# The second row of q is added by the DMA that loads it, in a pooled attention and gated FFN kernel

## Chip, cores and metric

The kernel runs on one core of one Trainium2 chip. The metric is the device time of one execution in microseconds. The engines are named as the profile names them: PE (TensorE, matmuls), DVE (VectorE), ACT (ScalarE), POOL (GpSimd) and SP (SyncE, which here issues DMAs and computes nothing). Each engine works through its own list of instructions in order; between engines there are only semaphores.

## What is computed

Attention over 4 batches of 8 heads, 1152 keys, head width 64. Two neighbouring queries are averaged first, so 576 pooled queries are left. Its output goes through a small network with a convolution of three taps as a gate. Cut to what matters:

```python
q_pool = q.reshape(B, H, S // 2, 2, D).mean(axis=3)
scores = q_pool @ k.T / sqrt(D)
attn = softmax(scores)            # with 1e-9 added to the sum
x = (attn @ v) -> (B, 576, 512)
h = relu(x @ w_in)                # 512 -> 1024
conv = w0 * h[t-1] + w1 * h[t] + w2 * h[t+1]
out = (h * sigmoid(conv)) @ w_out # 1024 -> 512
```

The change touches the first of these lines: the mean of two neighbouring rows of q, which the kernel makes as a sum (the factor is folded into a later scale).

## The kernel before

The 32 heads are worked on as 16 pairs (`Pair`, two heads share the 128 partitions). For each pair, `loads` brings in k, q and v from DRAM with DMAs that SP issues. q lies in DRAM in a layout in which the two queries of a mean stand as two rows of 640 columns beside each other, so one load fills the tile `qin` of 128 x 2 x 640 floats. There is one copy of `qin` in on-chip memory (`r_qin` has one slot), so a pair's load can start only when the pair before has been read.

`sum_q` (L299) adds row 1 of `qin` into row 0; it is a task of POOL, or of DVE where the table `SWAPPED` names it. Then ACT reads row 0 three times: `keep_q` (L302) makes `qt`, and two `turn_q` (L306) make `qd`, the copy with the two halves of the partitions exchanged. The score matmuls (L455) read `qt`, `qd` and `kt`.

`softmax` handles five blocks of 128 queries for each pair, with two score tiles for each of the first four and one for the last: 144 tiles in all, two of which fit in PSUM. For each tile: PE makes the scores (L455), DVE the row maximum (L467), ACT the exponential with its sum (L472), ACT or DVE the denominators (L485, L489), DVE the reciprocal (L495). Then the probabilities are scaled and split into two f16 halves: the high half on ACT (L519) or POOL (L514), the low half on DVE (L522), and a DMA transposes them (L535). For a few heads the scaling keeps f32 (L553 on ACT, L557 on POOL or DVE) and PE transposes (L571), ACT copies (L576). `values` multiplies with v (L601, L607), and v itself is split beforehand (L387 on POOL, L392 on ACT, L395 on DVE). `feed` is the first layer with relu, taps and gate (L691 to L725), `second` the second layer (L899 to L911) and its store. The weights come as 64-bit words and are decoded at the start and along the way by `weights` (L988 to L1044).

The order of all this is not made by dependences but by hand-carried tables: every step is a `Task`, `ORDER` lists the numbers of all 2484 tasks in the order in which they are emitted (so every engine's own order follows from it), `SLOTS` says which copy of a buffer each taker uses, and `SWAPPED` which tasks go to their second engine.

Of the kernel before, what the change touches and what calls it, by code (L numbers as in the profile page):

```python
# [94 lines left out]
cYaacXcZc2c4bNauc3c5c0abacadaehTafagc6ahc7c8hWhUc9bOdnc1aihVhXavibajawbPhYaEaxdmayiehZh0azh8ich1aAh9dbh2idaBia  # L95
h6ifh3aCitaFigaGdadqdJaHihiwdsiiaIaDiuiqh4dtakdrdOaJixijh5dHaKd0h7aLiyikirimdciLaMalivamanddaoaNiOapaOdKaqdGiz
ardLiAiMilasdMioiniBatdfiPiIipaYiNiEiJaPi3dNaQiFd1dgaRiQiKdhaSiGdiaTiRaZiSi4iCi0aUjrisdja0dka1i1iDi5a2i6joiTi7
dla3iHjba4iWjpi2d4iUiXjsjeiVdejqiYa5aVjtjGaWiZjJjui8jva6jHjDjcbijfd6jgaXi9a7jKjIjajEd5a8dobjjYdpjwjLjFbkbljdj1
bmjMjhd7bnjNjzjZbojVeneGjBjAjCjxj2jOjkjya9jWduj0bpj3babbdvj4j5bckdbqjTbdkgbrkedwbEjXkjjUkhj6bejPjldxeqjRkkjQki
dzdAbfj7klkybgdBj8dCdDjSj9kzdEkberkTkmdFkAkndIkvkUkfbFkWkBkakokwkLkceskCbGkXkDetbheHbHd8kGdykVbskEkHkMkIkJbtkY  # L100
kxlbbubIbvkZbJbyk0lek1lck8krkKdPkFkpksbwlfkqktd3k6kufAldk9k2bKltbxlglabQk3lwdQbRlhbSk7k4lilubTljkPbAbUlqlxbVk5
lvdRlrdSb5bCbzlolylslLbDlplzlOkQlAbLlMlIlBdTlmb6dUeKlPlElnlFlClkdVlDb7lNlJlGlQl3b8lKdWb9lHlRmolScalldXlTl0l4ep
# [1113 lines left out]
```

## Time and profile before

| | us |
|---|---|
| runs of the kernel before | 639.64, 641.41, 645.65 (median 641.41) |
| the execution that was profiled | 639.12 |
| its span, from first to last instruction | 637.3 |
| PE busy in it | 579.9 |
| DVE busy | 578.0 |
| ACT busy | 522.2 |
| POOL busy | 170.9 |

The span is the time between the first and the last instruction of the profiled execution; 1.8 us of its time lie around the span. "Busy" is the time in which an engine executes something other than register, semaphore and DMA-issuing instructions. An engine that waits is not busy, but an engine that is not the bottleneck may wait at no cost, so the shares are read stretch by stretch.

### The profile page before, as it was taken

The page shows a single profiled execution, that of the slowest core. Times are in us where ns is not written, and L with a number is a line of the kernel's source. Part 1 is how long each engine was busy: PE and PEld are TensorE (multiplying, and loading weights), DVE is VectorE, ACT ScalarE, POOL GpSimd, SP SyncE. Part 2 cuts the span into 40 slices and gives each one's busy share as a digit, 9 for nine tenths or more (in the row PEclk, how much of TensorE's full clock was granted, in tenths as well). Part 3 has the DMA queues.
Part 4 walks back from the last instruction along what each step waited for, and adds up shares of the span by engine and source line. Part 5 has one row for each costly group of instructions (what it writes and reads, how often), then busy time and mean ns, then how long its engine had stood idle before and what let it go on. Part 6 is the DMA issues. An engine that isn't in the chain of part 4 may idle for free. (4 is left out here: it accounts for less than half of the span.)

```text
span 637.3 us, 11886 instructions
## 1 busy us (share of the span) xinstructions
PE 579.9 (91%) x4411; PEld 361.6 (57%) x4411; DVE 578.0 (91%) x934; ACT 522.2 (82%) x982; POOL 170.9 (27%) x170
## 2 busy tenths in 40 slices
PE   3768888889999899999999899999999889999897
PEld 1435554556666565546666566475566536667753
DVE  5999999999999999989998999999999999987871
ACT  6999999969998888877888898678878788966761
POOL 0342434441313321033221211423121311231110
PEclk9779999889999999999999999999999999999999
DMA  7899696956386698999997999999999988988601
GB/s 271 257 185 197 163 213 144 209 119 140 84 191 163 159 185 166 189 186 188 221 199 170 225 191 178 176 209 189 191 166 239 180 144 159 197 135 133 90 34 42
DMA packets 276970, 109.63 MB, mean 172 GB/s; under 512 B 264880, under 2 KB 265904, under 8 KB 276912
## 3 DMA queue, kind: packets, MB, share of 16 engines
q1 hardware_dynamic: 276912, 108.87, 83.4%
q8 instruction: 35, 0.57, 0.4%
q14 instruction: 23, 0.19, 0.1%
HBM read 37.77 MB, written 4.72 MB: 67 GB/s over the span
## 5 line engine op out<-in xcount | busy, mean ns | idle before, releaser
L455 PE MATMUL s<-kt,qt 64*128 64x512 f32 (+3 forms) x704 | 190.5, 488 | 29.1 <-ACT p L472 20.2
L472 ACT ACTIVATE p<-s,sm 128x1152 f32<-128x1152 f32 x144 | 175.3, 1218 | 33.4 <-DVE sm L467 17.5
L467 DVE TENSOR_REDUCE sm<-s 128x1 f32<-128x1152 f32 x144 | 192.7, 1347 | 6.6 <-PE s L455 6.4
L522 DVE SCALAR_TENSOR_TENSOR hl<-p,sm,hl 128x1152 f16<-128x1152 f32 (+1 forms) x116 | 165.6, 1435 | 7.5 <-ACT hl L519 4.7
L455 PEld LDWEIGHTS s<-kt,qt 64*128 64x128 f32 (+1 forms) x704 | 91.9, 178 | 133.0 <-issue 80.2
L455 PE MATMUL s<-kt,qd 64*128 64x512 f32 x256 | 147.4, 657 | 0.0
L514 POOL TENSOR_SCALAR hl<-p,sm 128x1152 f16<-128x1152 f32 (+1 forms) x50 | 72.5, 1450 | 185.0 <-DVE sm L495 132.1
L601 PE MATMUL a<-pt,v 128*64 128x256 f16 (+2 forms) x1566 | 119.7, 272 | 1.9 <-DMA pt<-hl 1.2
L691 PE MATMUL a<-x,wi 128*128 128x257 f16 (+3 forms) x864 | 105.3, 274 | 4.6 <-ACT pt L576 1.5
L519 ACT ACTIVATE hl<-p,sm 128x1152 f16<-128x1152 f32 (+1 forms) x66 | 82.2, 1251 | 21.1 <-DVE sm L495 13.5
L601 PEld LDWEIGHTS <-v 128*64 128x64 f16 x1566 | 91.2, 110 | 11.3 <-issue 4.8
L691 PEld LDWEIGHTS <-wi 128*128 128x128 f16 x864 | 76.9, 98 | 30.6 <-issue 10.3
L905 PE MATMUL a<-wo,g 128*128 128x512 f32 x160 | 74.0, 602 | 0.4 <-DVE vs L353 0.4
L715 DVE SCALAR_TENSOR_TENSOR g<-h,cw,g 128x255 f32<-128x255 f32 (+3 forms) x144 | 68.8, 497 | 4.4 <-ACT g L704 3.9
L607 PE MATMUL a<-pt,v 128*64 128x256 f32 (+1 forms) x252 | 64.1, 409 | 0.7 <-ACT pt L576 0.7
L571 PE MATMUL a<-ident,p 128*128 128x128 f32 (+1 forms) x315 | 48.7, 281 | 15.2 <-POOL p L557 4.8
L576 ACT ACTIVATE pt<-a 128x384 f32<-128x384 f32 (+2 forms) x98 | 44.6, 475 | 7.3 <-PE a L571 7.3
L571 PEld LDWEIGHTS a<-ident,p 128*128 128x128 f32 (+1 forms) x315 | 32.8, 144 | 29.3 <-ACT pt L576 9.3
L905 PEld LDWEIGHTS a<-wo,g 128*128 128x128 f32 x160 | 28.7, 190 | 30.4 <-issue 28.4
L708 POOL TENSOR_SCALAR g<-h,cw 128x255 f32<-128x255 f32 (+3 forms) x26 | 22.5, 868 | 74.9 <-ACT h L697 53.3
L697 ACT ACTIVATE h<-a,bs 128x257 f32<-128x257 f32 (+3 forms) x72 | 33.6, 470 | 9.5 <-PE a L691 6.3
L557 POOL TENSOR_SCALAR p<-p,sm 128x1152 f32<-128x1152 f32 (+1 forms) x17 | 24.5, 1444 | 58.9 <-DVE sm L495 42.8
(134 smaller groups left out, 668.1 us busy)
## 6 DMA issues: line engine op xcount, KB each, us to landing
qin<-in_q_dram SPq DMA_DIRECT2D x15, 640.0 KB, 4.9
kt<-in_k_dram SPq DMA_DIRECT2D x16, 576.0 KB, 5.5
vin<-in_v_dram SPq DMA_DIRECT2D x9, 576.0 KB, 4.1
g<-in_moe_w_in_dram SPq DMA_DIRECT2D x8, 512.0 KB, 5.1
w<-in_moe_w_out_dram SPq DMA_DIRECT2D x8, 512.0 KB, 4.1
out_dram<-o SPq DMA_DIRECT2D x16, 256.0 KB, 2.7
vin<-in_v_dram SPq DMA_DIRECT2D x7, 288.0 KB, 3.2
v<-in_v_dram SPq DMA_DIRECT2D x7, 288.0 KB, 3.5
```

Of the source, the lines that this page charges most:

```text
L455: nc.tensor.matmul(out=w, lhsT=f, rhs=kk, start=True, stop=True)
L467: nc.vector.tensor_reduce(out=sm[:, e:e + 1], in_=runs(st[e]), axis=AX.XY, op=ALU.max, negate=True)
L472: nc.scalar.activation(out=p.tile().rearrange("p (a n) -> p a n", a=2), in_=runs(st[e]), func=AF.Exp, bias=sm[:, e:e + 1], scale=1.0, accu ...
L514: eng.tensor_scalar(out=hl[rows, 0], in0=ps_[e][rows], scalar1=sm[rows, 6 + e:7 + e], scalar2=1.0, op0=ALU.mult, op1=ALU.mult,)
L519: nc.scalar.activation(out=hl[rows, 0], in_=ps_[e][rows], func=AF.Copy, scale=sm[rows, 6 + e:7 + e])
L522: nc.vector.scalar_tensor_tensor(out=hl[rows, 1], in0=ps_[e][rows], scalar=sm[rows, 6 + e:7 + e], in1=hl[rows, 0], op0=ALU.mult, op1=ALU.s ...
L571: nc.tensor.transpose(w[:, (i - a1) * nq:(i - a1 + 1) * nq], ps_[e][rows, i * P:(i + 1) * P], ident[rows, rows])
L601: nc.tensor.matmul(out=to, lhsT=o.v[:, e, c, vc:vc + D], rhs=o.pt[y, e][:, hl * NC + c, 0:n], start=(c == 0 and j == 0), stop=(c == NC - 1 ...
L607: nc.tensor.matmul(out=to, lhsT=o.v[:, e, c].bitcast(F32), rhs=p32.rearrange("p (a n) -> p a n", a=NC)[:, c, 0:n], start=(c == 0), stop=(c ...
L691: nc.tensor.matmul(out=w[:, 0:n], lhsT=wi[:, a, j, f * P:(f + 1) * P], rhs=x.x[:, c, s0:s0 + n], start=(i == 0 and j == 0), stop=(i == 2 a ...
L715: nc.vector.scalar_tensor_tensor(out=c, in0=h[:, t:t + tok], scalar=cw[:, f, t:t + 1], in1=c, op0=ALU.mult, op1=ALU.add)
L905: nc.tensor.matmul(out=w.tile(), lhsT=g[f // 4][:, f % 4, c:c + P], rhs=wo[:, f, :], start=(f == 0), stop=(f == FC - 1),)
```

## The change

For pairs 1 to 15 SP now loads only row 0 of q (320 KB instead of 640 KB). The sum is no instruction of DVE or POOL any more: POOL issues a DMA that loads row 1 and adds it to row 0 in on-chip memory. Pair 0, whose q comes in two parts at the very start, keeps its two loads and sums. The tables `ORDER`, `SLOTS` and `SWAPPED` are new throughout, since the order was searched again. In `split_out`, which borrows `qin` late in the program, the shape of the borrowed tile is written in another way; its instructions are the same.

```diff
         def load_q(cols):
-            nc.sync.dma_start(
-                out=o.qin.tile()[:, :, cols], in_=q[o.pr].rearrange("p (r n) -> p r n", r=2)[:, :, cols]
-            )
+            rows = q[o.pr].rearrange("p (r n) -> p r n", r=2)
+            if o is pairs[0]:
+                nc.sync.dma_start(out=o.qin.tile()[:, :, cols], in_=rows[:, :, cols])
+            else:
+                nc.sync.dma_start(out=o.qin.tile()[:, 0, cols], in_=rows[:, 0, cols])
...
+        def add_q(cols):
+            nc.gpsimd.dma_start(
+                out=o.qin[:, 0, cols], in_=q[o.pr].rearrange("p (r n) -> p r n", r=2)[:, 1, cols], accum_op=ALU.add
+            )
...
-            t = add("POOL", 0.2 + 1.32 * n / K0, lambda eng, cols=cols: sum_q(eng, cols), after=[lq[i]], uses=[o.qin],
-                    port=True, alt=("DVE", dve(n), True))
+            if o is pairs[0]:
+                t = add("POOL", 0.2 + 1.32 * n / K0, lambda eng, cols=cols: sum_q(eng, cols), after=[lq[i]], uses=[o.qin],
+                        port=True, alt=("DVE", dve(n), True))
+            else:
+                t = add("POOL", 1.1, lambda sum_q=add_q, cols=cols: sum_q(cols), after=[lq[i]], uses=[o.qin], dma=1.5)
...
-cYaacXcZc2c4bNauc3c5c0abacadaehTafagc6ahc7c8hWhUc9bOdnc1aihVhXavibajawbPhYaEaxdmayiehZh0azh8ich1aAh9dbh2idaBia
+cYaacXc2cZc4auc0dmbNabc1c3acc5adaehTafagc6ahc7c8hWaihUc9avdnajhXhVaEawhYibaxayhZh0h8h1ieicbOdbh9idh2dqazh6iaif
```

How many instructions of each kind stand on an engine before and after, counted in the two built programs (kinds that are not listed are equal; lines are those of the kernel before):

| engine | kind | before | after |
|---|---|---|---|
| POOL | sum of q L299 | 9 | 0 |
| POOL | DMA with add, issued | 0 | 15 |
| POOL | scalings L514, L557 | 50, 17 | 53, 20 |
| POOL | split of v L387 | 6 | 9 |
| POOL | L625, L708, L793, L838 | 12, 26, 1, 1 | 9, 25, 3, 0 |
| DVE | sum of q L299, 640 columns | 7 | 0 |
| DVE | sum of q L299, pair 0 (384 columns; after 256 too) | 1 | 2 |
| DVE | denominators L489 | 27 | 40 |
| DVE | scaling L557 | 13 | 11 |
| ACT | denominators L485 | 53 | 40 |
| ACT | scaling L519 | 66 | 63 |
| ACT | split of v L392 | 10 | 7 |
| ACT | L553, L789, L834 | 5, 5, 3 | 4, 3, 4 |
| ACT | L623, L704 | 24, 46 | 27, 47 |
| PE | all | 6236 | 6236 |
| SP | DMAs issued | same number | same number |

Three places in the orders. The names in the rows are tiles, with the number of the buffer; the changed file has nine more lines ahead of the functions concerned, so L302, L306, L472, L514 and L557 of before read L308, L312, L481, L523 and L566 in it.

POOL, early in the program, before: five instructions around the first of its 640-column sums (pair 3).

```order
L514 TENSOR_SCALAR hl_290<-p_232,sm_205 128x1152
L514 TENSOR_SCALAR hl_341<-p_319,sm_274 128x1152
L557 TENSOR_SCALAR p_356<-p_356,sm_335 64x1152
L299 TENSOR_TENSOR qin_315<-qin_315 128x640
L383 MEMSET vs_162 64x1
```

And in the changed program, POOL's first two DMAs (pairs 1 and 2) and what stands between them.

```order
L566 TENSOR_SCALAR p_132<-p_132,sm_124 128x1152
L300 DMA qin_128<-in_q_dram 128x640
L410 MEMSET x_176 128x2x2
L1033 TENSOR_TENSOR wo_68<-g_91,wo_68 128x512
L523 TENSOR_SCALAR hl_215<-p_185,sm_155 128x1152
L566 TENSOR_SCALAR p_161<-p_161,sm_155 128x1152
L410 MEMSET x_228 128x2x2
L300 DMA qin_220<-in_q_dram 128x640
```

Pairs 1 and 2, which DVE summed before, now have their DMA in POOL's list, each behind a scaling L566.

DVE, before, around the sum of pair 1.

```order
L467 TENSOR_REDUCE sm_157<-s_148 128x1
L992 TENSOR_SCALAR g_142<-g_142 128x512
L299 TENSOR_TENSOR qin_123<-qin_123 128x640
L1001 TENSOR_SCALAR wo_68<-g_142 128x512
L495 RECIPROCAL sm_157<-sm_157 128x2
```

The same place in the changed program (the weights' steps L992 and L1001 read L1000 and L1009 there, the maximum L476).

```order
L1000 TENSOR_SCALAR g_135<-g_135 128x512
L476 TENSOR_REDUCE sm_188<-s_179 128x1
L1009 TENSOR_SCALAR wo_68<-g_135 128x512
L1000 TENSOR_SCALAR o_98<-o_98 128x512
L1014 SCALAR_TENSOR_TENSOR wo_68<-g_134,wo_68 128x512
L504 RECIPROCAL sm_155<-sm_155 128x2
```

The sum has left DVE's list, and a row maximum and a step of another weight have moved up into the place.

ACT, before, from the last read of pair 1's `qin` (the first row) to the first read of pair 2's (the last row).

```order
L302 ACTIVATE qt_217<-qin_123 128x640
L576 ACTIVATE pt_178<-a_209 128x3x128
L1016 ACTIVATE g_141<-g_141 128x512
L576 ACTIVATE pt_178<-a_173 128x3x128
L472 ACTIVATE p_232,sm_205<-s_196,sm_205 128x1152
L338 ACTIVATE x_189,vs_162<-v_125 128x576
L988 ACTIVATE g_215<-g_214 128x512
L472 ACTIVATE p_250,sm_205<-s_181,sm_205 128x1152
L1044 ACTIVATE g_142,ws_69<-wo_68 128x512
L1016 ACTIVATE g_214<-g_214 128x512
L485 ACTIVATE sm_205<-sm_205 128x2
L302 ACTIVATE qt_271<-qin_225 128x640
```

In the changed program, the rows between the last read of pair 1's `qin` and the first of pair 2's (an L312 of `qin_220`, which follows the last row here).

```order
L347 ACTIVATE x_176,vs_158<-v_101 128x576
L481 ACTIVATE p_225,sm_188<-s_192,sm_188 128x1152
L585 ACTIVATE pt_202<-a_169 128x3x128
L585 ACTIVATE pt_202<-a_208 128x3x128
L996 ACTIVATE g_205<-g_204 128x512
L585 ACTIVATE pt_202<-a_232 128x3x128
L1024 ACTIVATE g_134<-g_134 128x512
L481 ACTIVATE p_253,sm_188<-s_179,sm_188 128x1152
L1024 ACTIVATE g_204<-g_204 128x512
L494 ACTIVATE sm_188<-sm_188 128x2
L1052 ACTIVATE g_135,ws_69<-wo_68 128x512
```

Ten instructions stood between the two reads and eleven stand there now: one copy of L576 (L585) has been added.

## Rows read from the trace of the kernel before

**Rows 1.** The page: the span, and part 1, busy us and share.

```profile
span 637.3 us, 11886 instructions
PE 579.9 (91%) x4411; PEld 361.6 (57%) x4411; DVE 578.0 (91%) x934; ACT 522.2 (82%) x982; POOL 170.9 (27%) x170
```

**Rows 2.** Busy time by stretch; last columns: PE's clock, DMA share, GB/s.

```profile
0.00:20.00 20.00, 9.28 (x32) 5.23 (x32) 12.30 (x21) 13.52 (x25) 2.93 (x9) 0.88 0.72 259
20.00:240.00 220.00, 191.54 (x1346) 122.11 (x1348) 212.20 (x344) 200.99 (x388) 77.15 (x72) 0.96 0.76 172
240.00:560.00 320.00, 308.37 (x2272) 187.91 (x2269) 301.18 (x450) 263.31 (x459) 77.95 (x77) 1.00 0.99 188
...
600.00:637.30 37.30, 32.90 (x313) 18.88 (x310) 18.05 (x57) 16.81 (x50) 3.73 (x6) 0.99 0.09 33
```

The engines in these rows stand in the order PE, PEld, DVE, ACT, POOL.

**Rows 3.** The same for line L299 alone, columns DVE and POOL.

```profile
20.00:240.00 220.00, 2.60 (x3) 10.55 (x6) 0.96 0.76 172
240.00:560.00 320.00, 3.27 (x4) 4.06 (x2) 1.00 0.99 188
```

**Rows 4.** Groups by line and form: busy us, mean ns of one, idle before.

```profile
L299 POOL TENSOR_TENSOR qin<-qin 128x640 f32<-128x640 f32 x8 | 14.6, 1826 | 12.6 <-DMA qin<-in_q_dram 10.3 <-ACT x L623 2.4
...
L557 DVE TENSOR_SCALAR p<-p,sm 128x1152 f32<-128x1152 f32 x9 | 8.3, 919 | 0.0
...
L299 DVE TENSOR_TENSOR qin<-qin 128x640 f32<-128x640 f32 x7 | 5.9, 838 | 0.1
...
L489 DVE SCALAR_TENSOR_TENSOR sm<-sm,small 128x2 f32<-128x2 f32 x23 | 3.6, 157 | 3.8 <-ACT p L472 3.7
...
L519 ACT ACTIVATE hl<-p,sm 128x1152 f16<-128x1152 f32 x62 | 77.2, 1251 | 21.1 <-DVE sm L495 13.5 <-issue 7.2 <-ACT xf L617 0.3
...
L485 ACT ACTIVATE sm<-sm 128x2 f32<-128x2 f32 x41 | 8.2, 201 | 0.5
...
L392 ACT ACTIVATE v<-vin,vs 128x576 f16<-128x576 f32 x5 | 3.9, 773 | 0.4 <-DVE vs L373 0.4
```

**Rows 5.** Waits: us in total, times, longest. First and last of six DVE rows.

```profile
PE s L455 <- ACT p L472: 20.2, 25, 2.5
...
DVE hl L522 <- ACT hl L519: 4.7, 4, 1.3
...
DVE g L725 <- ACT g L721: 2.8, 5, 1.1
```

**Rows 6.** DMA issues: times, KB each, median us from issue to landing.

```profile
qin<-in_q_dram SPq DMA_DIRECT2D x15, 640.0 KB, 4.9
...
vin<-in_v_dram SPq DMA_DIRECT2D x7, 288.0 KB, 3.2
...
qin<-in_q_dram SPq DMA_DIRECT2D x1, 256.0 KB, 3.4
```

**Rows 7.** Line L265, the loads of q: ns of one issue; us to landing.

```profile
L265 SPq DMA_DIRECT2D qin<-in_q_dram x17: 327/532/1434, 0.7 to 441.6; - x17
...
DMA to landing us min/median/max: 3.4/4.9/6.4
```

**Rows 8.** Timeline of pair 2's q: start us, us, what [idle before].

```profile
24.62 0.74 ACT L302 ACTIVATE qt<-qin 128x640 f32<-128x640 f32 x1
...
25.39 0.33 SPq L265 DMA_DIRECT2D qin<-in_q_dram  x1
...
31.13 0.82 DVE L299 TENSOR_TENSOR qin<-qin 128x640 f32<-128x640 f32 x1
...
31.42 0.20 ACT L485 ACTIVATE sm<-sm 128x2 f32<-128x2 f32 x1
...
31.98 0.74 ACT L302 ACTIVATE qt<-qin 128x640 f32<-128x640 f32 x1 [0.36 <-DVE qin L299]
```

**Rows 9.** Timeline of POOL, two of its L514.

```profile
58.94 1.23 POOL L514 TENSOR_SCALAR hl<-p,sm 128x1152 f16<-128x1152 f32 x1 [7.35 <-DVE sm L495]
...
322.58 2.69 POOL L514 TENSOR_SCALAR hl<-p,sm 128x1152 f16<-128x1152 f32 x1 [1.89 <-DVE sm L495]
```

More of the change, by code (lines that the diff above doesn't have):

```diff
@@ new lines @@
+daaAitaFaBigaGiuaCihiwdsaHaDbPaIh3akdth4iiaJixiqdrdcdHd0ijiyirduh7h5ikalddimilamaKandfdKiLivaoapaLaqdgizaMiOdh
+araNiAasaOiodMiMiIatiniBaYiPdLdGipiJiCiQaPdii3iKiNaQaRdjaSiRaZaTiDiGa0isaUa1iSdki4i0iEdNjoi5a2i1d1iTjra3jpi2iF
+i6a4iWiHi7jsiXi8iYjqiUa5deeujtjGjba6juiZjJaVd4iVa7dljebijHaWjcjfjgjvi9aXjda8jKjDjIjad6jEdodpjYd5jhjwjLjZjzjBjA
+j1bja9bkjMjxbljCbad7jkjNbbj0bmenjFj2jOjVbndvjWbojybpeqj3bcjTkgbqjldwbdj4j5kjjUkhj6brjRbebEjPkdkkjXjSjQkidxkedz
+j9kykadAdJklbfkfj7kzbgkbeskTj8dBkAdCdDkmkndEembFkWkvdFbGdIbHbIbhkLbJkwkckBetbskCkUkDkGerkEdykVkJkXkokFkKkMkHbK
@@ new lines @@
+btkYlbeHbukxbLbvbwlekZk0lck8bykplfk1kIkqkrktk9dOkskuk2lgk6bzlaldltbxk3lwk7bQbClhbRkPlibSdPlulqbTdQbUljdRlrbVlv
+lxb5k4fAkQd3k5lslmbDlydTlLdUlnlzdVlAlOdWlIlMlBlob6dXbMbAlPlClplDlGeKlkb7lHlJlQlEd8b8lNlKl3b9calRmolScbl4lTlFll
+mpl5dYlUlYdSccl6mrlZl0dZcdlWlVl7l1eMbWmgd2mqgbmsl8eNeLbBmte1l2l9mGbXmhbYlXmJmbmud9mvmHmamcmweamemdmfebmKmDmImx
+mzbZmAmEmymBedmLmYb0mFmCeem1b1mMefb2egmNmZmOekm0mPb3mTehngmUb4mVm2eicemRkNmQe3ejmkm3mWeoepjimim4nhjmmXcfkOkRjn
+mSm5mjcgnjjjmlm6nichm7ndnkm9m8mmnbcinynlnee5nTnmcjnfnakSe4nnelnLnznockevnUecncnvnAcle6nwewnpnMnWcmnqnVexnNcwnB
@@ new lines @@
+nCnrnOnXnGnDntobnsnEnuDHnYocnFDtcxDIcyeGmnnxDfDunZczn0cAn1D2n4DJcBn2DgD3n9cCn5oeDhoan6cDodDKn7ofcEnJn8DvnHDiot
+ogcnDLn3DjDwnIowouohD4DkDMDmnKD5ovoifiD6DNDlDVDnoxomojoLDxDookconPDWDpoycpolDqcqD7oMDrfkDXozDyoAcroBeJcsDzctoC
+opnQoOoqcuoNDsoroPcvonnRo3osoooEcFoQoDezDYoJeADOfmoRoSnSoKo4oToWDAeBoUDPDQoZDBcGD9eCDCeDeEDRDDo0cHo5oXDEprD8cI
+oYo6cJfnpoo7eFEaoHDSeIppo8o1oVoIo2oFDFpgeycKpqpbpsEbcLePcMDGoGcNptpGo9cOphpuflpJpvpapHpwpepcpKpzpfpdEgpIpxeOcP
+pApYEhcQpypBEcpLDZpEcRpZpCEip1pDDTEjfBp0fUpMpkpNEde0p2pOD0eQpRpPpFcSp3pQEkfDp4p5D1qgp6p9cTElpWp7plcUqaqypXqhp8
@@ L140 @@
+KrAsC0KsLuLmBIC1LcBJAtBKLdAuKtzuC2KVBLC7AvKpLeKuzvBVKWAwKJC8LnLvAxC9LfDbDaKKKLLwAyLxKMDcLgLyLELzBMKNLoKOLSLhLF
+BNLCLGLZLHLTKvKPLILALDLLL0LJL6L1DdLMDeLKLNLBLUAHL7LVBWL2AIAJLOL8LPMdL3LQLWBXBYLXMrL4LYL9MeMaMkBZMbL5MfMsMcNAAK
+MlMtMuM8MgNBMyLRMvM9NaMhMwNHNfMiMmNCMxNbNgNcNIMnMGNEMjNDMoMHNdNhMIMpNiNLMqNFNjNJNkNGMzNMMAMBNKNeMCMUNNMVMEMDM1
+MWNOMJM2MFNRNPMKMXM3NQM4MNM5MYM6NSMZM0MOMLMPMMNVNmMQMRM7NTMSNnNoNpMTNqNtNlNrNYNUNZNuNvNwNxN2NWNyNXNzNsN3N0N1N4
 N5N8N6N7N9OaObOcOd
@@ L280, in loads @@
             lq.append(add("SP", 0.3, lambda cols=cols: load_q(cols), uses=[o.qin] if lq else [],
-                          takes=[] if lq else [o.qin], dma=2.3 * (cols.stop - cols.start) / K0))
+                          takes=[] if lq else [o.qin], dma=(2.3 if o is pairs[0] else 1.15) * (cols.stop - cols.start) / K0))
         es = slice(two[0], two[-1] + 1) if two else None
@@ L815, in view @@
             t = bufs[j].tile()
-            names = " ".join("abcd"[:len(t.shape) - 1])
-            if len(t.shape) > 2:
-                t = t.rearrange(f"p {names} -> p ({names})")
+            if bufs[j].ring is not r_w and bufs[j].ring is not r_kt:
+                t = t.rearrange("p a n -> p (a n)") if bufs[j].ring is r_qin else t.rearrange("p a c d -> p (a c d)")
             return t.bitcast(F16)[:, 0:4 * DM].rearrange("p (a f n) -> p a f n", a=2, f=2)
```

98 lines of the change are left out of this document (39 added, 59 removed).

## The prediction

> **What bounds the kernel now.** First the busy shares of the whole execution [rows 1]: PE 579.9 us, DVE 578.0, ACT 522.2 of a span of 637.3; GpSimd has 170.9. Two engines at 91% each are not yet a bound, so next comes the view by stretches [rows 2]. From 20 to 240 us DVE is busy 212.20 of 220 us (96%) and PE 191.54 (87%): here DVE sets the pace. From 240 to 560 us PE is busy 308.37 of 320 (96%) and DVE 301.18 (94%): here PE leads by little, and only 11.6 us of the stretch have no matmul. After 600 us DVE is busy 18.05 of 37.3 us and PE 32.90, so PE alone has the end. The reader is to see that a microsecond taken from DVE is worth a microsecond in the first of these stretches, part of one in the second, and nothing in the last. GpSimd bounds nothing anywhere (27% of the span).
>
> The third view is the waits [rows 5]. PE stands 20.2 us before score matmuls because ACT has not yet read the score tile (the exponential, L472), and DVE waits for ACT in six kinds of places from 4.7 to 2.8 us, 22.9 us together. So ACT is not the bound, but it ends many of the small waits of the two engines that are.
>
> **The change, part by part.** The sum of 15 pairs leaves two engines. Of these sums, GpSimd had 8 at 1.83 us (14.6 us) and DVE had 7 at 0.84 us [rows 4]. GpSimd's saving is worth nothing by itself: it was not the bound, and it now issues 15 DMAs in their place. What an issue from GpSimd takes no row shows; the nearest rows are SP's own issues, 0.33 to 1.43 us [rows 7]. I take 1.0 us, so 15 us come back for the 14.6 that go.
>
> DVE's 7 sums fall 3 in the DVE-bound stretch (2.60 us) and 4 in the PE-bound one (3.27 us) [rows 3]. The first count in full: -2.6 us. Of the second I count half, since PE leads there by only 2% of the stretch: -1.6 us. The table of orders also moves small work. DVE takes 13 of the denominators (L489) at 0.157 us from ACT, +2.0 us; it loses two scalings (L557) at 0.92 us, -1.8 us; and the 256-column sum of pair 0 comes to it in the start, where DVE waits for loads anyway [rows 2, 4]. Net +0.2 us. Everything else on DVE is the same instructions in another order. Together -4.0 us.
>
> ACT loses more: 13 of L485 at 0.201 us, three scalings L519 at 1.25, three of L392 at 0.77, so 2.6 + 3.8 + 2.3 = 8.7 us [rows 4]; its other moves cancel. I count this at zero in the sum, since ACT has slack (201 of 220 us, 263 of 320 [rows 2]), and keep it for a rival. PE's instructions are the same.
>
> What the change adds is a longer way for q. Before, one load of both rows lands and one sum makes it ready. Now a load of 320 KB lands, GpSimd sees that and issues the second load, that lands with its add, and only then may ACT read. The buffer qin has one copy, so the way starts only when ACT has finished reading the pair before. The place where this is tightest is pair 2, and it was the tightest before too: ACT ends its reads of pair 1 at 25.36 us, SP issues the load at 25.39, DVE sums at 31.13, and ACT reads at 31.98 after a wait of 0.36 us [rows 8]. Between, ACT ran ten instructions, to 31.62: 6.3 us of cover. In the changed order the same ten stand there and one more copy of L576, some 0.45 us, so 6.7 us of cover.
>
> The way in it: the half load. 256 KB of q landed 3.4 us after issue, 288 KB of v 3.2 [rows 6]; I take 3.4. The issue on GpSimd, 1.0. Then the adding load, of which no row shows the like. At least it is a load of its size, 3.2 us; at most, since it reads two operands for each that it writes, I take the slowest landing of any q load, 6.4 us [rows 7]. Between these I take 4.0, nearer to the plain load, because it moves 320 KB from memory and the rest stays on the chip. That makes 8.4 us, 1.7 more than the cover. Bounds: 3.2 + 0.3 + 3.2 = 6.7, no wait, and 3.5 + 1.4 + 6.4 = 11.3, a wait of 4.6.
>
> Queued behind ACT's waiting read are the exponentials, which PE's next score tile and DVE's row sums wait for; in the DVE-bound stretch ACT has about 9% of slack, so I count the wait whole. For the other pairs, ACT's work between SP's load and its first read, added up by the same durations, is 9.0 us (pair 1), 9.3 (3), 9.9 (10), 10.1 (4) and 11 to 24 for the rest. At 8.4 us none of them waits; at 11.3 they add 2.3 + 2.0 + 1.4 + 1.2 = 6.9 us. SP's queue keeps its number of issues, and it is relieved of half of q's bytes.
>
> GpSimd's issue also stands in front of scalings that DVE waits for, and waits itself for the load. It waits for DVE far longer than that today, and DVE hardly ever for it, so I count nothing; what it costs if that cover is gone is the rest of the load, up to 3.4 us at a place, once or twice.
>
> There is a row that speaks against the issue from GpSimd. The same 128x1152 scaling takes GpSimd 1.23 us in one place and 2.69 in another [rows 9]: something beside it holds it up by as much as 1.5 us. If an issue is held like that, pair 2 waits 3.2 us instead of 1.7, and pair 1, 3 and 10 begin to wait (0.9 + 0.6 + 0.0), so some 3 us more. The Trainium skill, SBUF — State Buffer, "SBUF: two separate sides", gives a reason for such rows: while DVE runs certain fast operations GpSimd can't write the descriptors of its DMAs, and the transfer seems blocked; its example is 620 ns that became 3100. By its figures the hold-up would be an estimated 2.5 us rather than 1.5. No run here shows this for a DMA. On the other side, the Trainium skill, DMA: Bandwidth & Descriptors, "Anatomy of one DMA — SWDGE (gpsimd) path", prices such a transfer at 2.0 us and its bytes at 436 GB/s, an estimate of 2.75 us here, and the wait at pair 2 would be 0.5 us by it.
>
> **The sum.** -2.6 - 1.6 + 0.2 + 1.7 = -2.3 us. The execution that was profiled took 639.1 us (its span is 637.3), so 636.8; I say 637. The median of the three runs is 641.4, and that execution lies at the lower edge of their 639.6 to 645.7, so the forecast is 0.7% under the median: by a measurement of this kernel about 1% is the least that can be told from no change.
>
> **The rivals.**
> *The shorter ACT pays too* (630 us). The new order leaves ACT 8.7 us less, and 20.2 us of PE's and 22.9 of DVE's waits end on ACT [rows 5]. If an eighth of these 43 us goes, and the adding load lands soon enough (a wait of 0), then 639.1 - 4.0 - 5.4 = 629.7. For it: in the first stretch ACT is busy 91% and the waits are many and short. Against: a shorter ACT queue does not help where ACT itself waited for DVE.
>
> *PE leaves nothing over* (640 us). If the PE-bound stretch gives nothing back, and the wait at pair 2 takes what the first gains: -2.6 + 0.2 + 1.7 = -0.7, so 638.4; with one or two waits on GpSimd of a microsecond, 640. For it: PE is busy 96% there. Against: DVE is only 2% behind it.
>
> *The adding load lands late* (648 us, the other side). With 11.3 us from SP's issue to the landed sum, the waits are 4.6 + 6.9 = 11.5 us and the time 639.1 - 4.0 + 11.5 = 646.6; with the hold-up of GpSimd's rows on top (1.5 us at five places that already wait) 654. I put it at 648. It decides from the point at which the waits reach the gain of 4.0 us, which is a way of about 9.7 us (3.0 at pair 2, 0.7 at pair 1, 0.4 at pair 3), so an adding load that lands 5.3 us after its issue. For it: a q load of twice the bytes took 4.9 us in the median, 6.4 at most [rows 6, 7], and the DMA engines are 76% to 99% busy [rows 2]. Against: these 4.9 us are for 640 KB.
>
> That the change does not do what it says is no rival: the sums are gone from DVE's and GpSimd's rows; only what they were worth is open.
>
> **How the numbers follow.** Forecast (634 to 641) 0.44; the shorter ACT (627 to 634) 0.24; nothing over (638 to 642) 0.10; late landing (645 to 660) 0.22. Faster by over 1% is below 635.0: the ACT case and 0.08 of the forecast, 0.32. Slower by over 1% is above 647.8: the late landing but its lower end, 0.20. Within 1%: 0.48. The range 629 to 650 leaves out about 0.05 at the bottom of the ACT case and 0.11 at the top of the late landing. Since cases of both signs hold much of the chance: the likeliest one's own range is 634 to 641.
>
> **What would show it.** In the profile of the changed kernel the sum's rows on DVE and GpSimd are two (pair 0), and DVE is busy about 573 us (-5), ACT about 513. The adding load's row gives its landing: 3.2 to 5 us supports the forecast, over 5.3 the late rival. ACT's wait for it at pair 2 should be 1 to 2 us and the only one of its kind; waits at pairs 1, 3 and 10 as well speak for the late rival. If PE's 20.2 us before score tiles shrink by 3 or more, the ACT rival holds. The prediction is wrong if the adding load's time is not near a load's, or if the new order makes waits that have nothing to do with q.

## The result, and the profile after

The changed kernel takes 644.98 us in the median of 20 runs (640.77 to 649.67), the kernel before 640.83 us in 20 runs beside it. The ratio is 1.0055, with a 95% interval of 1.0036 to 1.0074: the change costs about 3.5 us. The forecast was 637.0 us, a small gain.

The profiled execution took 645.68 us, of it a span of 643.8 us. First its span and busy times on the page [rows 1].

```profile
span 643.8 us, 11933 instructions
...
PE 577.1 (90%) x4411; PEld 361.9 (56%) x4411; DVE 571.5 (89%) x939; ACT 513.1 (80%) x965; POOL 167.5 (26%) x182
```

DVE has 6.5 us less to do than before, ACT 9.1 us less, and the span is 6.5 us longer (these two executions lie further apart than the medians, which are 4.2 us apart). So engines stand where they didn't. By stretch (columns as in [rows 2]):

```profile
20.00:240.00 220.00, 187.01 (x1340) 120.68 (x1338) 209.43 (x346) 198.01 (x382) 75.22 (x74) 0.97 0.80 172
240.00:560.00 320.00, 302.93 (x2215) 184.79 (x2210) 291.77 (x450) 253.72 (x443) 71.95 (x78) 0.99 1.01 183
```

From 240 to 560 us PE is busy 302.93 us and DVE 291.77, against 308.37 and 301.18. The start of the 73rd row maximum is at 281.6 us (before: 280.8), that of the 97th at 385.6 (before: 375.3). Not all of these 9.5 us come from q: in the same order without the second row (first experiment below) the two start at 279.7 and 378.2, so there 4 us of them open as well, and 5.5 come with the adding load. By the last tile the changed kernel is 5.8 us behind the one before.

What an issue of the adding load (L300) takes, what it waited for and who waited for it, in the view of that line, with its landing:

```profile
L300 POOL DMA_DIRECT2D qin<-in_q_dram x15: 875/895/1029, 16.8 to 448.3; - x15
...
  DMA qin<-in_q_dram: 13.0, 4
...
  ACT qd L312: 6.7, 2
...
DMA to landing us min/median/max: 4.7/5.8/9.9
```

GpSimd takes 0.9 us for an issue, and stood 13.0 us at four of them for the half load. ACT waited twice for the sum, 6.7 us together. The timeline shows the two places. Pair 2 first (start, duration, engine, line; in brackets the wait):

```profile
24.27 0.74 ACT L308 ACTIVATE qt<-qin 128x640 f32<-128x640 f32 x1
25.03 0.33 SPq L268 DMA_DIRECT2D qin<-in_q_dram  x1
29.72 0.89 POOL L300 DMA_DIRECT2D qin<-in_q_dram  x1 [3.39 <-DMA qin<-in_q_dram]
34.47 0.63 ACT L312 ACTIVATE qd<-qin 64x512 f32<-64x512 f32 x1 [2.03 <-DMA qin<-in_q_dram]
```

That is the wait that was forecast (1.7 us; it is 2.03). The other is pair 12's:

```profile
345.70 1.23 POOL L523 TENSOR_SCALAR hl<-p,sm 128x1152 f16<-128x1152 f32 x1 [4.80 <-DVE sm L504]
346.87 0.90 POOL L300 DMA_DIRECT2D qin<-in_q_dram  x1
...
350.81 1.25 ACT L528 ACTIVATE hl<-p,sm 128x1152 f16<-128x1152 f32 x1
...
356.76 0.63 ACT L312 ACTIVATE qd<-qin 64x512 f32<-64x512 f32 x1 [4.70 <-DMA qin<-in_q_dram]
...
360.26 0.56 DVE L724 SCALAR_TENSOR_TENSOR g<-h,cw,g 128x321 f32<-128x321 f32 x1 [6.20 <-ACT g L713]
```

GpSimd's scaling L523 waits 4.80 us for DVE, so the adding load behind it is issued only at 346.87; it lands 9.9 us later, the longest of the 15. ACT waits 4.70 us, and DVE, whose next operand comes from ACT behind that read, 6.20.

How it comes to land late, the transposing DMAs of the probabilities (`pt<-hl`, issued by SP) tell in part. The first line is their landing in the kernel before, the second in the changed one, all 125 of them; the third, in the changed one too, is that of the two issued at 343.8 and 349.5 us, around pair 12's adding load.

```profile
DMA to landing us min/median/max: 4.0/4.9/8.6
```

```profile
DMA to landing us min/median/max: 3.9/5.2/13.2
```

```profile
DMA to landing us min/median/max: 9.3/11.2/13.2
```

So SP's transfers are late there too. In the ten traces of this document without loads from GpSimd, the slowest transpose lands after 8.5 to 9.0 us; in the six where 15 pairs use the adding load, after 10.4 to 15.8. The adding loads that land late (8.7 us at pair 8, 9.9 at pair 12) have a transpose in flight that is as late (9.3 and 13.2). So the very late transposes come with loads from GpSimd. That the two delay each other is the likely reading; why some of them are so late and others not is not shown.

### The profile page after: what moved, and what is told of

It is laid out like the page before. It is cut to its first block, busy times and chain, and to the rows that moved or that the text cites. A ratio compares the mean times of both kernels' runs of the same rounds, so it can differ in the third digit from the quotient of the medians.

```text
span 643.8 us, 11933 instructions
## 1 busy us (share of the span) xinstructions
PE 577.1 (90%) x4411; PEld 361.9 (56%) x4411; DVE 571.5 (89%) x939; ACT 513.1 (80%) x965; POOL 167.5 (26%) x182
## 5 line engine op out<-in xcount | busy, mean ns | idle before, releaser
L464 PE MATMUL s<-kt,qt 64*128 64x512 f32 (+3 forms) x704 | 187.9, 487 | 29.4 <-ACT p L481 20.9
L481 ACT ACTIVATE p<-s,sm 128x1152 f32<-128x1152 f32 x144 | 175.2, 1217 | 47.4 <-DVE sm L476 27.8
L476 DVE TENSOR_REDUCE sm<-s 128x1 f32<-128x1152 f32 x144 | 192.5, 1346 | 4.5 <-PE s L464 4.2
L464 PE MATMUL s<-kt,qd 64*128 64x512 f32 x256 | 145.3, 650 | 0.0
L523 POOL TENSOR_SCALAR hl<-p,sm 128x1152 f16<-128x1152 f32 (+1 forms) x53 | 73.8, 1394 | 225.5 <-DVE sm L504 158.6
L610 PEld LDWEIGHTS <-v 128*64 128x64 f16 x1566 | 92.4, 110 | 12.2 <-issue 6.2
L700 PEld LDWEIGHTS <-wi 128*128 128x128 f16 x864 | 77.2, 98 | 33.0 <-issue 12.2
L528 ACT ACTIVATE hl<-p,sm 128x1152 f16<-128x1152 f32 (+1 forms) x63 | 78.7, 1251 | 14.4 <-DVE sm L504 10.9
L585 ACT ACTIVATE pt<-a 128x384 f32<-128x384 f32 (+2 forms) x98 | 43.8, 472 | 5.2 <-PE a L580 5.1
L566 POOL TENSOR_SCALAR p<-p,sm 128x1152 f32<-128x1152 f32 (+1 forms) x20 | 26.5, 1323 | 58.2 <-DVE sm L504 41.1
L717 POOL TENSOR_SCALAR g<-h,cw 128x321 f32<-128x321 f32 (+3 forms) x25 | 17.3, 690 | 86.9 <-ACT h L706 75.9
## 6 DMA issues: line engine op xcount, KB each, us to landing
kt<-in_k_dram SPq DMA_DIRECT2D x16, 576.0 KB, 5.0
vin<-in_v_dram SPq DMA_DIRECT2D x9, 576.0 KB, 4.8
```

Source lines behind the costliest of these rows:

```text
L464: nc.tensor.matmul(out=w, lhsT=f, rhs=kk, start=True, stop=True)
L476: nc.vector.tensor_reduce(out=sm[:, e:e + 1], in_=runs(st[e]), axis=AX.XY, op=ALU.max, negate=True)
L481: nc.scalar.activation(out=p.tile().rearrange("p (a n) -> p a n", a=2), in_=runs(st[e]), func=AF.Exp, bias=sm[:, e:e + 1], scale=1.0, accu ...
L523: eng.tensor_scalar(out=hl[rows, 0], in0=ps_[e][rows], scalar1=sm[rows, 6 + e:7 + e], scalar2=1.0, op0=ALU.mult, op1=ALU.mult,)
L528: nc.scalar.activation(out=hl[rows, 0], in_=ps_[e][rows], func=AF.Copy, scale=sm[rows, 6 + e:7 + e])
L610: nc.tensor.matmul(out=to, lhsT=o.v[:, e, c, vc:vc + D], rhs=o.pt[y, e][:, hl * NC + c, 0:n], start=(c == 0 and j == 0), stop=(c == NC - 1 ...
```

## The experiments

"New order" is the changed kernel's, "old order" that of before. The expectations name three theories: L, the adding load lands late and ACT waits for it; O, the new order stalls by itself; C, the DMAs that GpSimd issues slow the other transfers. In the table after the last experiment stand all medians, ratios and DVE's busy time.

### What the second row costs in the new order

**Second row left out.** `add_q` issues nothing; the half load stays.

```diff
-            nc.gpsimd.dma_start(out=o.qin[:, 0, cols], in_=..., accum_op=ALU.add)
+            pass
```

> The changed kernel with q's second row left out: the first row is loaded, nothing is added, ACT reads at once. What the new order costs with nothing of the adding load left. L: 637 to 638. O: 645. C: 638.

638.28 us (0.9954), as L and C had it. This is all that the new order can gain: 3.0 us.

**Loaded, but not added.** The same load from GpSimd goes into row 1, without an add.

```diff
-                out=o.qin[:, 0, cols], in_=..., accum_op=ALU.add
+                out=o.qin[:, 1, cols], in_=...
```

> The changed kernel, but GpSimd's DMA loads the second row into row 1 of qin and adds nothing (the sum is left out), so nobody waits for it; the issues and their bytes stay. L: 638. O: 645. C: 645. The landing of this plain load beside that of the adding one (median 5.8 us) tells what the add itself costs: if the add is slow, 3.5 to 4.5 us here; if the issue from GpSimd or the full DMA engines are slow, still 5 to 6.

640.68 us (0.9983). Between the expectations. ACT waits for q nowhere. So 15 issues and their bytes cost 2.4 us by the medians, 1.9 by the ratios, with nobody waiting for q. That is hardly more than the intervals (0.0024 and 0.0018 to either side), the granted clock was 0.982 in the mean of these runs and 0.986 in those without the second row, and in the two profiled executions all tiles start within 0.8 us of each other: a cost of the issues is likely, not shown. The other 4.6 us up to the changed kernel are the add, the waits for it, and one thing more that this edit takes away: into row 1 GpSimd loads without waiting for the half load, for which it stood 13.0 us in the changed kernel. The landings in the view of the line:

```profile
L300 POOL DMA_DIRECT2D qin<-in_q_dram x15: 584/587/809, 16.6 to 441.0; - x15
...
DMA to landing us min/median/max: 3.2/4.5/8.0
```

With the add the median is 5.8 us, so the add makes a landing some 1.3 us longer.

**Old sum in the new order.** All pairs load 640 KB and are summed on GpSimd again, at the places of the adding loads (the line below stands in two functions).

```diff
-            if o is pairs[0]:
+            if True:
```

> The changed order, with q loaded whole (640 KB) and summed by GpSimd as before; no DMA adds. The kernel before runs at about 641, the changed one at 645. Theory L (the adding load lands late and ACT waits for it, 2.0 us at pair 2 and 4.7 at pair 12 in the profile): 638, since the waits go and DVE keeps its relief. Theory O (the new order stalls by itself, whatever q does): 645. Theory C (the DMAs that GpSimd issues slow the other transfers): 638 too.

653.87 us (1.0191): every theory missed. The page:

```profile
PE 576.5 (89%) x4411; PEld 360.7 (55%) x4411; DVE 585.9 (90%) x939; ACT 514.1 (79%) x965; POOL 181.6 (28%) x182
```

DVE has the same 939 instructions as in the changed kernel, and is busy 14.4 us longer. A sum on GpSimd lengthens what DVE does beside it. Once seen, it is there in the kernel before too (timeline of two engines):

```profile
126.02 1.55 POOL L299 TENSOR_TENSOR qin<-qin 128x640 f32<-128x640 f32 x1
...
126.14 2.64 DVE L522 SCALAR_TENSOR_TENSOR hl<-p,sm,hl 128x1152 f16<-128x1152 f32 x1
```

That form has a mean of 1437 ns there; beside the sum it took 2.64 us. Worked out from the trace (each DVE instruction that overlaps a sum, against the shortest quarter of its form): in the kernel before 4 of GpSimd's 8 sums do this, 5.2 us together; here 13 of 15, 14.6 us. All four of before and ten of the 13 have two operands in on-chip memory; the other three are steps of the weights (L1000, L1018) with one. The Trainium skill, SBUF — State Buffer, "Who interferes with whom", has the rule: a DVE instruction with two SBUF inputs contends with a GpSimd instruction that reads SBUF. The trace agrees for the 14 with two operands, at 0.5 to 1.36 us for each; of the three with one that sentence says nothing. Which of the two began first matters: three L522 that ran already when a sum of the kernel before came kept their 1.40 to 1.41 us, and the sums took 2.41, 1.77 and 2.45 us instead of 1.55.

### The wait at pair 12

**Pair 12 earlier.** Its half load and its adding load go 76 and 51 tasks ahead of ACT's first read, 22 places earlier for the latter.

```diff
+            if o.pr == 12:
+                plan.early += [(lq[i], ready, 76), (t, ready, 51)]
```

> The changed kernel with one thing moved: pair 12's load and its adding load stand 6 and 22 places earlier in the order, 51 places ahead of ACT's first read instead of 29. L: ACT's wait of 4.7 us at pair 12 goes and the time falls by 3 to 5, to 640 to 642. O and C: 645, no change.

642.02 us (1.0012), the upper end of what L named; the slowest landing is 7.7 us, and ACT waits 0.7 us for q in all. By the ratios this one wait was worth 2.8 us of the loss, give or take 1.8.

**Two halves, from pair 2 on early.** The two rows of `qin` become two buffers by turns; from pair 2 on, load and adding load stand 75 and 45 tasks ahead.

```diff
-                nc.sync.dma_start(out=o.qin.tile()[:, 0, cols], in_=rows[:, 0, cols])
+                nc.sync.dma_start(out=pairs[0].qin[:, o.pr % 2, cols], in_=rows[:, 0, cols])
...
+            if o.pr >= 2:
+                plan.early += [(lq[i], ready, 75), (t, ready, 45)]
```

> The changed kernel with qin's two rows used as two buffers in turn (a pair's sum grows in row 0 or row 1), and from pair 2 on each load placed 75 and each adding load 45 places ahead of ACT's first read, so that no read should wait. L: 637 to 638. O and C: 645.

642.23 us (1.0005, 0.9978 to 1.0032). L's 637 to 638 missed. ACT waits for the adding loads nowhere any more, and the kernel is level with that before, not faster: 3.2 of the 4.6 us come back, and what is left over the load without add (1.4 us) is no more than the intervals tell.

### The old order with the adding load

**Old order, adding load for all 15.** The tables of before, with the adding load where each sum stood.

> The order of the kernel before with the adding load in the place of each sum (on GpSimd's list for all 15 pairs). There ACT's first read follows the sum of pairs 1, 2, 10 and 14 at once. L: four waits of some 5 us and shorter ones elsewhere, 655 to 665. O: the order was the fault, so at most 641.

650.74 us (1.0142), below what L named and above O's. The whole loss lies ahead of the 25th tile (112.2 us instead of 99.0): ACT waits 4.74 us at pair 1, 6.33 at pair 2, 0.96 at pair 3, 12 us together; at pairs 10 and 14, of which L expected some 5 us each, it waits 0.2 and 0.4. One landing took 15.4 us (pair 8), and nobody waited for it.

**The same without the second row.** `add_q` issues nothing.

> The order of the kernel before with the sums and the second row of q left out: what the sums cost there. By the prediction's term for DVE (2.6 + 1.6 us, without the moves of the new table) 636 to 637; if the sums were hidden behind PE, 640 to 641.

634.81 us (0.9885). That is under the 636 to 637 expected: the old order has 7.4 us to gain from the sums, not the 4.2 of the forecast, and it is 4.4 us better than the new one without them by the ratios.

**Two halves early in the old order**, and **only pairs 1 to 3 early** (43, 52, 64 tasks ahead for the load, 21, 30, 36 for the adding load), both with the edit of two halves as above.

> The order of the kernel before, adding loads in the place of the sums, qin's rows as two buffers, and loads and adding loads 75 and 45 places ahead of ACT's first read. L: near e7 (637), faster than the kernel before. O: 637 too. C: 641 to 645, since the DMAs from GpSimd still disturb the rest.

> The order of the kernel before with the adding load in the place of each sum, qin's rows as two buffers in turn, and only the first three pairs' loads moved: the adding loads of pairs 1, 2 and 3 to 21, 30 and 36 places ahead of ACT's first read, loads of pairs 2 and 3 to 52 and 64. In e6 ACT lost 12.0 us at these three places and 0.9 elsewhere. Theory L+P (late landing at three places is all that makes the old order slow with the adding load, and what the sums cost there, 7.3 us by e7, is then gained, less some 2 us for GpSimd's issues as e3 against e2): 636 to 639, faster than the kernel before by 0.5 to 0.8%. Rival C (the adding DMAs cost more by slowing what runs beside them): 641 or more.

649.89 us (1.0144) and 648.34 us (1.0096): both missed. In the first, pair 1 (not moved) still waits 4.95 us, and GpSimd, whose queue is in order, now stands for half loads with other work behind it (the list of waits):

```profile
POOL qin L307 <- DMA qin<-in_q_dram: 31.4, 8, 15.3
...
POOL hl L532 <- DMA pt<-hl: 21.3, 3, 10.0
```

A second loss of 8.4 us opens there between the row maxima at 426.4 and 438.6 us, and by the waits it comes from late transposes, not from these stands: an adding load and a transpose, both issued at 418.8, land after 11.8 and 12.3 us, PE waits 5.4 us for transposes, ACT 9.2 for PE, DVE 9.2 for ACT. In the other, 2.21 us of wait are left at pair 2, 0.79 at pair 10 and 2.50 at pair 14 (436.8 us), and 3.2 us open near 170 us. There too an adding load and a transpose were issued together, at 159.8, and landed after 11.0 and 11.2 us; a load of weights behind them took 8.9 us (before: 3.9), and ACT stood 3.5 us for it. So theory C, too, has a part in what the adding loads cost.

**Both orders side by side**, without the second row, in the same rounds on one chip.

> The changed kernel without the second row of q (that part of the computation is left out), on the same chip and in the same rounds as the old order without it. In separate rounds it took 0.9954 of the kernel before and the old order 0.9885, 4.4 us apart. If the new order is by itself the worse one, they are 3 to 5 us apart here too. If that came from comparing across chips, they are within 1.5 us.

> The old order without the second row of q (that part of the computation is left out), beside the new order without it. If the old order is by itself the better one: 0.9885 of the kernel before again, 3 to 5 us under its neighbour. If that came from comparing across chips: within 1.5 us of it.

638.58 us (0.9955) and 635.37 (0.9904): 3.2 us apart, as expected if the new order is by itself the worse one. DVE is busy 570.4 us in the one and 568.1 in the other, so 2.3 of the 3.2 us are work of DVE.

### What a sum costs in the old order

**GpSimd's eight sums left out, DVE's seven sums left out**; all 640 KB loads stay. The second has `nc.vector` in this line.

```diff
+            if eng is nc.gpsimd and o is not pairs[0]:
+                return
```

> The kernel before with only those 8 sums left out that GpSimd does in whole (pairs 3 to 7, 9, 11, 15; both rows are still loaded, DVE keeps its 7). GpSimd is 27% busy. Theory P (a sum on GpSimd stretches the DVE instruction beside it, by 5.2 us in all in the profile of before): DVE's busy time falls by 5 us and the time by 2 to 5, to 636 to 639. Rival: GpSimd is never the bound, so nothing changes, 641.

> The kernel before with only DVE's 7 sums left out (pairs 1, 2, 8, 10, 12, 13, 14). By the prediction's terms 2.6 + 1.6 us: 637. If e7's gain of 7.3 us came from these alone: 634 to 635. With e12 it divides that gain between the two engines.

636.56 us (0.9920), as theory P had it, and 639.50 us (0.9968), above both expectations. GpSimd's sums, counted at nothing, cost 5.1 us; DVE is busy 4.8 us less without them (573.2). DVE's sums, 5.9 us of instructions, gave only 2.1 us. DVE's busy time says why: it fell by 2.0 us, not by 5.9. GpSimd's sums shifted against DVE's work and now meet five instructions instead of four (6.5 us instead of 5.2), and a few other forms took longer.

**All sums on DVE**, in the old order and in the new one (where all pairs load 640 KB again, as in "Old sum in the new order").

```diff
+            if o is not pairs[0]:
+                eng = nc.vector
```

> The kernel before with the eight sums of GpSimd given to DVE at the same places; nothing else changes, nothing is left out. Theory (GpSimd's sum costs the kernel about 0.6 us each because it holds up DVE's two-operand instructions beside it, and a sum on DVE costs about 0.3 us): 641 - 5.1 + 8 x 0.30 = 638.3 us. Rival 1 (a sum on DVE costs its whole 0.84 us where DVE sets the pace): 641 - 5.1 + 8 x 0.84 = 642.6. Rival 2 (the sums cost what they do because q becomes ready later, wherever they run): 640 to 641, no difference.

> The changed kernel's order with the 640 KB load of both rows, and all 15 sums as instructions of DVE; nothing is left out. With the sums on GpSimd the same order took 653.9 us, without them 638.3. Theory (of these 15.6 us nearly all come from GpSimd's sums beside DVE's instructions): 638.3 + 15 x 0.30 = 642.8 us, and DVE's l-halves and gates at their durations without sums. Rival 1 (a sum on DVE at its whole 0.84 us): 638.3 + 12.6 = 650.9. Rival 2 (the new order stands its loads of q too late for 640 KB and a sum, on whichever engine): about 652.

641.95 us (1.0010) and 650.77 us (1.0145). My price of 0.30 us for a sum on DVE, taken from the run before, falls in both; the whole price comes near (642.6 and 650.9 expected by it). In the new order the row reads

```profile
L307 DVE TENSOR_TENSOR qin<-qin 128x640 f32<-128x640 f32 x15 | 12.3, 818 | 2.5 <-DMA qin<-in_q_dram 2.5
```

12.3 us of sums cost 12.2 to 12.5 us. Ahead of 240 us, where 8 of them stand, the tiles fall 6.4 us behind those without sums, after it 5.8. In these 5.8 are DVE's waits for the 640 KB loads (1.69 us at 246.1 and 0.59 at 419.0), so 7 sums of 5.7 us cost 3.5 to 5.8 us in the stretch that I had called PE-bound. In the old order it is otherwise: against the run without GpSimd's sums, the six ahead of 240 us put the tiles 6.0 us behind, and the two after it 0.1. What a sum on DVE costs in the PE-bound stretch, these runs do not settle.

### The adding load only where it pays

**Four pairs, eight pairs, seven pairs**, in the old order: adding load, issued where GpSimd's sum stood, for pairs 6, 9, 11, 15 (whose sums lengthened DVE's work), for all eight that GpSimd summed, and for these without pair 3 (whose sum met nothing and whose adding load ACT waited for 1.66 us). All others keep load and sum of before. The line below is that of seven, against the one with all 15.

```diff
-            if o is pairs[0]:
+            if o.pr not in (4, 5, 6, 7, 9, 11, 15):
```

> The order before; only pairs 6, 9, 11 and 15, whose sums on GpSimd lengthen an instruction of DVE (5.2 us together), get the half load and the adding load, issued where the sum stood; the other eleven pairs keep 640 KB and their sums. Nothing is left out. Theory (DVE's busy time counts nearly in full in this kernel, whichever engine makes it): 641 - 5.2 + 4 x 0.15 for the issues + about 0.5 of waits = 637 us, DVE busy about 573. Rival 1 (the four remaining sums of GpSimd move and meet DVE's instructions as those did, as happened when DVE's sums were left out): 640 to 642, DVE busy 576 to 578. Rival 2 (the adding load's waits eat what is gained, as with all 15): 643 or more.

> The order before; all eight pairs that GpSimd summed (3, 4, 5, 6, 7, 9, 11, 15) get the half load and the adding load, issued where the sum stood; the seven pairs that DVE summed keep 640 KB and their sums. Nothing is left out. Without these eight sums the kernel took 636.6 us. Theory: 636.6 + 8 x 0.13 for the issues + 0.96 for pair 3's wait + 0.6 for others = 639.2 us, DVE busy about 573. Rival 1 (the issues that stand on GpSimd waiting for a half load hold the scalings behind them): 643 or more. Rival 2 (nobody waits for them in these places, pair 3 neither): 637.5.

> As with eight adding pairs in the old order (638.3 us), but pair 3 gets its 640 KB and its sum on GpSimd back: its adding load was the only one that ACT waited for (1.66 us at 53.7 us), and its sum meets no instruction of DVE in the kernel before. Nothing is left out. Theory (a wait of ACT for q is paid whole, and a sum of GpSimd that stretches nothing costs nothing): 638.3 - 1.66 - 0.13 = 636.5 us. Rival (the wait at pair 3 is made up later, or the sum now meets a DVE instruction): 638 to 639.

639.73 us (0.9967), 638.33 (0.9951) and 637.02 (0.9936, 0.9918 to 0.9954). With four, pair 7's sum, left on GpSimd, met an instruction of DVE that it had missed before (1.28 us), and DVE stayed at 575.7. With eight, no sum of GpSimd is left behind pair 0. With seven, no wait of ACT for q of pairs 3 to 15 is left, and no lengthened instruction:

```profile
PE 576.7 (91%) x4411; PEld 360.1 (57%) x4411; DVE 573.4 (90%) x934; ACT 522.2 (82%) x982; POOL 164.5 (26%) x170
```

The slowest transpose lands after 8.7 us, as in a kernel without loads from GpSimd. By the ratios this version is 4.1 us faster than the kernel before and 7.6 us faster than the changed one. The step from eight to seven (1.3 us) lies within the intervals.

All runs; the last column is the median less DVE's busy time of the one profiled execution:

| kernel | us | ratio, 95% | DVE busy | rest |
|---|---|---|---|---|
| before | 641 | 1 | 578.0 | 63 |
| old order, all sums on DVE | 641.95 | 1.0010 (0.9987-1.0033) | 579.5 | 62 |
| old, DVE's sums out | 639.50 | 0.9968 (0.9945-0.9992) | 576.0 | 64 |
| old, GpSimd's sums out | 636.56 | 0.9920 (0.9898-0.9943) | 573.2 | 63 |
| old, no second row | 634.81 | 0.9885 (0.9857-0.9912) | 568.1 | 67 |
| the same, beside the new | 635.37 | 0.9904 (0.9873-0.9936) | 568.1 | 67 |
| old, 4 adding | 639.73 | 0.9967 (0.9947-0.9987) | 575.7 | 64 |
| old, 8 adding | 638.33 | 0.9951 (0.9930-0.9971) | 572.7 | 66 |
| old, 7 adding | 637.02 | 0.9936 (0.9918-0.9954) | 573.4 | 64 |
| old, 15 adding | 650.74 | 1.0142 (1.0098-1.0185) | 569.8 | 81 |
| old, two halves, pairs 1-3 early | 648.34 | 1.0096 (1.0061-1.0131) | 569.9 | 78 |
| old, two halves early | 649.89 | 1.0144 (1.0098-1.0191) | 567.6 | 82 |
| new, no second row | 638.28 | 0.9954 (0.9930-0.9978) | 570.9 | 67 |
| the same, beside the old | 638.58 | 0.9955 (0.9934-0.9975) | 570.4 | 68 |
| new, load without add | 640.68 | 0.9983 (0.9966-1.0001) | 570.9 | 70 |
| new, all sums on DVE | 650.77 | 1.0145 (1.0109-1.0181) | 582.2 | 69 |
| new, all sums on GpSimd | 653.87 | 1.0191 (1.0163-1.0218) | 585.9 | 68 |
| new, adding load (the change) | 644.98 | 1.0055 (1.0036-1.0074) | 571.5 | 73 |
| new, pair 12 early | 642.02 | 1.0012 (0.9992-1.0033) | 571.5 | 71 |
| new, two halves early | 642.23 | 1.0005 (0.9978-1.0032) | 572.8 | 69 |

As long as nobody waits for q, the time follows DVE's busy time nearly one for one within an order, whichever engine makes it longer: the rest is 62 to 64 us in the old order with sums and 67 to 69 in the new one. Without any sum it is 67 in the old order too; that PE, busy 579 to 582 us, keeps some of the gain there is argued, not shown. What the adding loads cost beyond DVE's time shows in the last column: 73 with the change, 78 to 82 in the old order with 15 of them (for "pairs 1-3 early" the profiled execution took 644.3 us, by which its rest is 74).

## Why the prediction was wrong, step by step

The sum was -2.3 us; the ratio says +3.5. By the ratios, on 641.4 us (each measured step is a difference of ratios, good to some 2 us):

| step | forecast | measured | from |
|---|---|---|---|
| sums leave DVE and GpSimd | -4.2 | -7.4 | old order, no second row |
| new order | +0.2 | +4.4 (3.2 side by side) | new less old, no second row |
| issues from GpSimd | 0 | +1.9 | load without add, less none |
| waits for q, with GpSimd's stands for the half load | +1.7 | +4.6 | change, less load without add |

**No single step turned the sign.** The sums gave 3.2 us more than was counted, and the order, the issues and the waits took 4.2 (3.0 side by side), 1.9 and 2.9 us more. With the waits as forecast the measured steps still add up to +0.6, with the order as forecast to -0.7. Two of these steps failed in what they said of the kernel: that no other pair waits, and that the moved small work is all that the new order costs.

**"At 8.4 us none of them waits."** Pair 2's wait was right: place, cause, and 2.03 us for 1.7 (half load to issue 4.7 us for 3.4, issue and adding load 4.7 for 5.0, cover 7.4 for 6.7); that it came so near is in part luck, since these three misses offset each other. What failed is the sentence on the other pairs. I counted their cover as ACT's work from SP's load to ACT's first read, as if GpSimd issued as soon as the half load is there. At pair 12 that cover is 14.1 us in the trace (338.01 to 352.06), and the half load was early (GpSimd did not wait for it), but the issue stood behind a scaling that waits for DVE: it went out at 346.87, and ACT ran dry at 352.06. In the trace ACT comes to its read 2.7 us after GpSimd's issue at pair 2, 5.0 at pair 1, 5.2 at pair 12, 6.8 at pair 3, and 7.8 or more at all others; I had not counted this distance. The landing did the rest: with its median of 5.8 us ACT would have waited 0.6 us at pair 12, with 9.9 it was 4.7, beyond the 7.8 us (1.4 for the issue, 6.4 for the landing) that I took as the upper bound. With that pair earlier the kernel is level with before.

**The rival with the late landing** had the sign, and of its mechanism the late landing, but not the places: it named pairs 1, 3 and 10, and none of them waits. That its 648 us lies near is partly luck: it counted 11.5 us of waits, where they took 4.6 and the order and the issues, in its sum at next to nothing, the rest. The landing by the profile's row, 5.8 us in the median from the start of the issue, leaves 4.9 behind the issue, under the 5.3 from which it was to decide. It told all the same, by one long landing at one place, since the gain that the waits had to eat up was smaller than the 4.0 us that I had set against them (3.0 with no second row at all, 1.1 after the issues). Its hold-up of GpSimd's issue did not come: none of the 15 took over 1.03 us. The rule that GpSimd can't write descriptors while DVE runs some operations (the Trainium skill, SBUF — State Buffer, "SBUF: two separate sides") does not show in these issues; no run tests it by itself, but where landings are long, SP's transposes, which GpSimd does not issue, are late as well. The 2.75 us estimated from the Trainium skill, DMA: Bandwidth & Descriptors, "Anatomy of one DMA — SWDGE (gpsimd) path", are too few for the adding load: its shortest landing is 4.7 us, 3.8 behind the issue. The plain load's shortest, 3.2 us from the start of the issue, comes near.

**"GpSimd's saving is worth nothing by itself" was wrong** by 5.1 us; DVE's seven sums, counted at 4.2, gave 2.1 when they alone were left out, so two misses offset each other in part. [Rows 4] already had a sign of it, a mean of 1826 ns for a sum, and [rows 9] another: engines that hold each other up. I read them as GpSimd's loss; the loss that counted was DVE's, in the rows of DVE beside the sums.

**Half price in the PE-bound stretch** is neither borne out nor refuted: with all sums on DVE, seven sums of 5.7 us there cost 3.5 to 5.8 us in the new order, and two cost 0.1 in the old one. Not all of DVE's time can be had at once: without any sum, 10 us of its busy time gave 6 to 7. So the rival that PE leaves nothing over is not decided either; its 640 us left out what the order, the issues and pair 12 cost.

**The moved small work at +0.2 was too small.** The denominators cost what was counted (12 more in the main form, 0.167 us each), and the scalings gave back what was counted (1.7 us). But the order as a whole cost 3.2 to 4.4 us, and DVE is busy 2.3 to 2.8 us longer in the new order without sums than in the old; two-operand forms grew there (the 64-row L522 from 1413 to 1550 ns), and I had only looked at what moved onto or off DVE, not at what each instruction stands beside. What DVE's instructions take above the lowest quarter of their form beside one of GpSimd is 7.9 us in the old order without sums and 8.5 to 9.5 in the new, so 0.5 to 1.5 us come from this. Where the rest of the new order's 3 to 4 us lies is open.

**Issues at nothing** cost 1.9 us, at the edge of what the runs can tell. GpSimd's own time was as counted (0.9 us for 1.0), so the loss, if it is one, lies elsewhere; where, is open. The transposes beside a load from GpSimd are a candidate: with the add the 125 of them land 5.50 us after issue in the mean, before 5.28.

**The rival of the shorter ACT** fell: ACT is busy 9.1 us less, as counted, and PE still stands for it before score tiles as before [rows 5]:

```profile
PE s L464 <- ACT p L481: 20.9, 26, 1.9
```

DVE busy 571.5 us and ACT 513.1 came close to the 573 and 513 named ahead; right busy times do not make a right sum.

## What to carry to other kernels

An asynchronous step that is put on an in-order queue is as early as its place in that queue lets it be: count its cover from the later of its input and what stands ahead of it there, for each place, and against the longest landing of a loaded stretch, not the median. Before you count work on an engine with slack as free, look at what the engine that sets the pace runs beside it, by the duration of single instructions against their form's usual one. And take such a change only where it pays: in the old order seven pairs gained 0.6%, and all fifteen lost 1.4%.

## What the runs showed of the hardware that was not expected

- A 128x640 f32 sum on GpSimd lengthens a two-operand DVE instruction that starts beside it by up to 1.36 us, nearly its own 1.55: 5.2 us over 8 sums before, 14.6 over 15 in the new order. Not only sums do this: in all 20 traces every DVE instruction that takes over 0.1 us more than the lowest quarter of its form overlaps one of GpSimd, 13.9 us together in the kernel before (4.5 of them beside the scalings L514) and 9.7 with the change.
- A load of 320 KB issued from GpSimd took 0.59 us to issue and 4.5 us to land in the median; with the add 0.90 and 5.8 (both from the start of the issue). SP's half loads landed after 3.3 to 4.3 us in the medians of the runs.
- Landings of the adding load spread widely: 4.7 to 9.9 us with the change, up to 15.4 in the old order with 15 of them. The latest ones had a transposing DMA of SP in flight that was as late: issued within 0.2 us of each other they landed after 15.4 and 15.8 us, 13.1 and 13.4, 12.1 and 12.7, 11.8 and 12.3, but elsewhere also after 6.8 and 8.0. Without loads from GpSimd no transpose took over 9.1 us.
